# One GpSimd product placed later and one normalization given to ScalarE in a hand-ordered linear-attention and MLP kernel

## The chip, the cores and the metric

The kernel runs on one core of a Trainium2 chip. A core has a matrix engine (TensorE, in the profile PE, with its weight loads as PEld), a vector engine (VectorE, DVE), an activation engine (ScalarE, ACT), a general engine (GpSimd, POOL) and a queue that issues the DMA transfers (SyncE, SP). Each engine takes its instructions strictly in the order in which they stand in its own queue, and waits at an instruction until what that instruction needs is there. The metric is the device time of one execution in microseconds (us).

## The reference, cut to what matters

The input is a sequence of 2048 rows of 512 numbers. It goes through a linear attention with 32 heads of 16, and then through a block of two mixers, each with its own layer norm:

```python
h = _layernorm(x) * (1 + ca) + sa
q, k, v = split(h @ wqkv)                       # 32 heads of 16
phi_q = concat(softmax(q @ w_phi), softmax(-(q @ w_phi)))
phi_k = concat(softmax(k @ w_phi), softmax(-(k @ w_phi)))
kv, z = phi_k^T v, sum(phi_k)
x = x + ga * ((phi_q kv) / (phi_q z)) @ wo
h = _layernorm(x) * (1 + cb) + sb
t = gelu(_layernorm(h) @ w1)                    # then four column groups shifted by +1, -1, +2, -2 rows
x1 = h + shifted(t) @ w2
x = x + gb * (x1 + gelu(_layernorm(x1) @ w3) @ w4)
```

## The kernel before

The 2048 rows are 16 tiles of 128 rows, and two tiles are a chunk of 256. All products run in float32 precision, each as three products of a rounded part ("hi") and a rest ("lo"). The program has three phases. The first makes the features of keys, values and queries, chunk by chunk, and writes the exponentials of the queries to DRAM. The second (`phase_a` and `mix`, chunk by chunk) reads these exponentials back, divides and scales them, multiplies them with the sum over the keys (`num`), multiplies with `wo`, normalizes, multiplies with `w1`, shifts, and multiplies with `w2`. The third is the wide MLP with `w3` and `w4` in blocks of 512 rows, by a scheme of Strassen's kind with seven products in place of eight.

The body of the program only makes a list of numbered steps. The sequence in which they are issued is written out by hand in the string `ORDER`: each word is a step's number, and a letter behind it says that the step runs on another engine than the one it was written for (G is GpSimd, V is VectorE, A is ScalarE). `Plan.order` reads it:

```python
for word in ORDER.split():
    o = self.ops[int(word.rstrip("AVG"))]
    if not word.isdigit():
        o.fn = o.alts[engines[word[-1]]][1]
    yield o
```

An engine's queue is what is left of this string when one keeps the words of that engine. Buffers are given out by hand too (`SLOT`): a step that fills a buffer waits until the last reader of what was in it before is done.

The steps that matter here, with their numbers in `ORDER` and the line of their code:

- In `q_phi`, tiles 10 and 11 of the queries' exponentials. VectorE makes the factors of both tiles (1234, line 943, `q<-q,pz`). Tile 11's exponentials are scaled by them on VectorE (1237, line 947, `e<-e,q`), tile 10's on GpSimd (1235, same line, same name). VectorE then transposes each of them in blocks (1238 for tile 11, 1236 for tile 10, `pT<-e`), 1236 writing into the buffer from which 1238 reads. Between these two stands 1066, the lo part of a transposed normalized chunk (`nT<-pt,nT`), whose TensorE transposes (`pt<-const,n`) come just before the `num` products of chunk 5 (`pp<-pT,const`).
- GpSimd's queue at that place: a power of -1/2 for a layer norm (1056, line 586, `rs<-mv,const`), the product of 512 columns of w4 with the row gb (1485, line 1129 in `load_w4`, `raw<-raw,gb`), 1235, two lo parts of w3 (1220 and 988, line 483, `ws`), and tile 12's product with the sum over the keys (1307, line 932, `ez<-e,const`), which is written into the buffer from which 1236 reads. The next step that reads the w4 product is a rounding on ScalarE (1492), far behind.
- In `layernorm2` (line 621), called by `normed(0)`: the first layer norm of the MLP, in which two tiles are normalized with their scale and shift and written in a mixed column order. One of the two is on ScalarE (1575), the other on VectorE (1574, `nb<-xl,rs,nm`), behind the transpose of tile 13's exponentials (1319) and in front of the block transpose of its own result (1576, `yt<-nb`). Behind that stand the factors of tiles 14 and 15 (1392 to 1396, `pz` and `q`) and the lo part of chunk 6's attention output (1323, `oT<-pp,oT`), which TensorE multiplies with `wo` (1327, 1328, `pp<-w,oT`).
- ScalarE's queue at that place: the GELUs of chunk 4, one of their roundings (1180, `sh<-gf`), a sum for the next layer norm (1584, `nb<-xl`), a square sum (1258, `n<-pp,nm`) and a small step (1585, `nm<-st`), which writes into the buffer of the scale that 1574 reads.

In the profile, L415 and L417 are a two-operand step on VectorE and on GpSimd, L398 is a step on ScalarE, L407 is the same scaling step on VectorE or GpSimd, L468 are the products, L477 the transposes of TensorE, and L691 the block transposes of VectorE.

Of the kernel before, what the change touches and what calls it, by code (L numbers as in the profile page):

```python
# [37 lines left out]
        "c2": ("st", "mv", "rs", "nm"), "c64": ("k1", "k2", "q1", "q5"), "c128": ("q2", "q3")}  # L38
TAG = {n: tag for tag, names in KIND.items() for n in names}
ORDER = (  # L40
# [1394 lines left out]
```

## Time and profile before

| | |
|---|---|
| time, median of 3 executions | 553.92 us (553.47 to 554.73) |
| the profiled execution, its own time | 556.63 us |
| its span, first to last instruction | 554.8 us |
| mean granted TensorE clock | 0.996 of full speed |
| busy share of the span: VectorE, ScalarE, GpSimd | 89%, 62%, 67% |
| DMA read and written | 89.74 MB, 34.35 MB |

The span is shorter than the time of the same execution by 1.83 us, which lie ahead of the first and behind the last instruction. In the rows of the profile a name such as `pp<-w,oT` is "written from read", by the program's names of the buffers; the number ahead of it is the start in us from the first instruction, then the duration in us; in brackets stands how long the engine had been idle and which instruction ended that.

### The profile page before, as it was taken

How to read it: one execution, taken by the hardware profiler on the slowest of the kernel's cores; microseconds unless marked ns; L12 is line 12 of the kernel's file. 1: busy time of each engine (PE TensorE's matmuls, PEld its weight loads, DVE VectorE, ACT ScalarE, POOL GpSimd, SP SyncE). 2: the span in 40 equal slices, each digit the busy share in tenths (PEclk: the TensorE clock that was granted, in tenths of full speed). 3: DMA queues.
4: the chain of work that ended last, by engine and by line, in shares of the span. 5: the costliest groups of instructions: out<-in, count | busy, mean ns of one | idle time of the engine just before them, and what ended most of it. 6: DMA issues, size and time to landing. Idle time of an engine off the chain costs nothing.

```text
span 554.8 us, 12326 instructions
## 1 busy us (share of the span) xinstructions
PE 544.5 (98%) x4509; PEld 487.4 (88%) x4509; DVE 495.5 (89%) x895; ACT 344.0 (62%) x807; POOL 371.9 (67%) x383
## 2 busy tenths in 40 slices
PE   9999999999999999899899999999999999999997
PEld 8788788888777887788689898999999999999997
DVE  4899999999999999999989987988889877988787
ACT  3799988844337888777788577874534345234430
POOL 3588977979699999889786265433665563345354
PEclk9999999999999999999899999999999999999999
DMA  8967155158545668856797899997659674592032
GB/s 308 385 219 259 78 191 175 50 167 272 146 121 191 229 205 278 281 186 217 239 294 277 296 312 332 372 365 247 273 128 420 230 278 160 171 344 113 1 116 76
DMA packets 64180, 124.89 MB, mean 225 GB/s; under 512 B 7060, under 2 KB 26772, under 8 KB 60024
## 3 DMA queue, kind: packets, MB, share of 16 engines
q1 hardware_dynamic: 63688, 123.91, 65.4%
q8 instruction: 35, 0.57, 0.4%
q10 hardware_dynamic: 432, 0.20, 0.1%
q14 instruction: 25, 0.20, 0.1%
HBM read 89.74 MB, written 34.35 MB: 224 GB/s over the span
## 4 chain that ended last, share of the span: by engine, by line
PE 48%; POOL 11%; DVE 10%; issue 2%; ACT 1%; DMA 1%; POOLq 0%; DVEq 0%; SPq 0%
PE pa L468 23%; PE ac L468 17%; PE pp L468 7%; POOL ez L417 3%; POOL e L417 3%; POOL qe L417 2%; DVE pT L691 1%; DVE pz L439 1%; DMA dram<-ws 1%; POOL ws L417 1%; DVE xb L415 1%; POOL rs L586 1%; DVE e L415 1%; DVE nb L407 1%; POOL sh L417 1%
## 5 line engine op out<-in xcount | busy, mean ns | idle before, releaser
L468 PE MATMUL pp<-w,hh 128*128 128x512 f32 x576 | 137.4, 396 | 0.2 <-DVE hh L415 0.2
L468 PEld LDWEIGHTS pp<-w,hh 128*128 128x128 f32 x576 | 106.9, 188 | 25.5 <-issue 1.0
L468 PE MATMUL pa<-bH,wq 128*128 128x256 f32 x840 | 105.5, 281 | 0.0
L468 PE MATMUL ac<-w,gg 128*128 128x256 f32 x840 | 105.4, 281 | 0.0
L468 PEld LDWEIGHTS ac<-w,gg 128*128 128x128 f32 x840 | 102.8, 188 | 1.2
L468 PEld LDWEIGHTS pa<-bH,wq 128*128 128x128 f32 x840 | 102.3, 188 | 0.6
L468 PE MATMUL pp<-w,oT 128*128 128x512 f32 x192 | 48.8, 405 | 1.8 <-DVE q L415 1.8
L417 POOL TENSOR_TENSOR gg<-cu,gg 128x128 fp32r<-128x128 f32 (+1 forms) x32 | 22.4, 707 | 39.6 <-PE ac L468 14.1
L468 PE MATMUL pp<-w,sh 128*128 128x512 f32 x192 | 48.3, 398 | 0.0
L468 PE MATMUL pa<-nT,w 128*128 128x256 f32 x384 | 47.0, 281 | 0.0
L468 PEld LDWEIGHTS pa<-nT,w 128*128 128x128 f32 x384 | 46.1, 188 | 0.8 <-issue 0.2
L468 PEld LDWEIGHTS pp<-w,oT 128*128 128x128 f32 x192 | 36.3, 193 | 10.4 <-ACT nb L398 2.2
L468 PEld LDWEIGHTS pp<-w,sh 128*128 128x128 f32 x192 | 35.3, 189 | 8.5 <-issue 0.8
L398 ACT ACTIVATE cu<-pa 128x512 f32<-128x512 f32 (+1 forms) x41 | 21.3, 524 | 29.7 <-PE pa L468 12.8
L586 POOL TENSOR_TENSOR rs<-mv,const 128x2 f32<-128x2 f32 x31 | 23.9, 770 | 18.3 <-ACT mv L593 18.0
L417 POOL TENSOR_TENSOR ez<-e,const 128x1024 f32<-128x1024 f32 x12 | 29.5, 2461 | 5.3 <-DVE pT L691 4.2
L398 ACT ACTIVATE gg<-cu 128x256 fp32r<-128x256 f32 (+1 forms) x48 | 16.5, 360 | 25.1 <-PE ac L468 22.6
L415 DVE TENSOR_TENSOR gg<-sg,gg 128x512 fp32r<-128x512 f32 x36 | 26.4, 738 | 4.1 <-ACT gg L398 2.9
L417 POOL TENSOR_TENSOR e<-e,q 128x1024 f32<-128x1024 f32 x15 | 29.2, 1969 | 0.0
L398 ACT ACTIVATE gg<-sg 128x512 fp32r<-128x512 f32 x28 | 17.3, 625 | 18.4 <-PE ac L468 6.8
L417 POOL TENSOR_TENSOR ke<-ke,k 128x1024 f32<-128x1024 f32 x14 | 28.4, 2025 | 0.0
L415 DVE TENSOR_TENSOR cu<-pa,cu 128x512 f32<-128x512 f32 (+1 forms) x36 | 21.0, 594 | 7.5 <-PE pa L468 5.8
(220 smaller groups left out, 1238.1 us busy)
## 6 DMA issues: line engine op xcount, KB each, us to landing
wq<-dram SPq DMA_DIRECT2D x32, 1024.0 KB, 8.2
dram<-ws SPq DMA_DIRECT2D x35, 256.0 KB, 3.5
dram<-qe SPq DMA_DIRECT2D x16, 512.0 KB, 3.0
e<-dram SPq DMA_DIRECT2D x64, 128.0 KB, 3.3
xl<-in_x SPq DMA_DIRECT2D x30, 256.0 KB, 4.5
raw<-in_w SPq DMA_DIRECT2D x18, 256.0 KB, 4.1
mod<-in_wmod SPq DMA_DIRECT2D x16, 256.0 KB, 4.7
dram<-xl SPq DMA_DIRECT2D x16, 256.0 KB, 3.0
```

The costliest lines, as they stand in the source:

```text
L398: nc.scalar.activation(o(), i(), func, **kw)
L407: other.append((e, c, lambda eng=eng: eng.tensor_scalar(o(), i(), get(s1), get(s2), op0=OP.mult, op1=OP.add), not isps(i) and not isps(o)))
L415: dve = ("DVE", 71 + 1.04 * o.n + 90 * (isps(a) and isps(b)), lambda: nc.vector.tensor_tensor(o(), a(), b(), op=op))
L417: pool = ("Pool", cost, lambda: nc.gpsimd.tensor_tensor(o(), a(), b(), op=op))
L439: plan.op("DVE", 65 + 1.04 * a.n + 110 * isps(o), lambda: nc.vector.tensor_reduce(o(), a(), axis=AX.X, op=op), [o], [a])
L468: nc.tensor.matmul(o(), a(), b(), start=s, stop=e, **kw)
L586: plan.op("Pool", 540 + 10 * m, lambda: nc.gpsimd.tensor_tensor(r(), v(), mhalf[:, :m](), op=OP.pow), [r], [v, mhalf])
L691: plan.op("DVE", 71 + 1.04 * o.n, lambda: nc.vector.transpose(o(), i()), [o], [i])
```

## The change

Only the string `ORDER` changes. Word by word many numbers trade places, but most of them do so across engines. Kept apart by engine, TensorE's and the DMA queue have the same sequence as before, and three queues differ by two moves:

- GpSimd: 1485, the w4 product, stood between 1056 and 1235. Now it stands behind 1235, 1220 and 988, and in front of 1307.
- VectorE and ScalarE: 1574, the normalization, loses its V. It is gone from VectorE between 1319 and 1576, and stands on ScalarE between 1180 and 1584.

```diff
-    "1090G 1230 874 1231 1055 1113 1108 1056 1232 1137 1114 1145 1485G 1058 600 1233 1063 995 1234 1139 1057 1237 "
-    "1059 1235G 1238 1064 1140 1065 1066 1220G 1236 1146 961 988G 965 1141 1307G 989 1060 1239 1305 1061 1240 1213 "
...
+    "1090G 1230 874 1231 1055 1113 1108 1056 1232 1137 1114 1145 1058 600 1233 1063 995 1234 1139 1237 1057 1059 "
+    "1235G 1238 1064 1140 1065 1066 1220G 1236 1146 961 988G 965 1141 1485G 989 1060 1305 1239 1061 1240 1213 1307G "
...
-    "1076 1075 1216 1183 1493G 1319 1175 1579 1083 1250 1179 1084 1180 1574V 1488G 1584 1576 1085 1258 1486G 1392 "
...
+    "1075 1216 1183 1493G 1319 1175 1579 1083 1179 1250 1084 1180 1488G 1085 1574 1486G 1086 1584 1576 1217G 1258 "
```

26 rows, old and new, of the table ORDER are left out of this document.

## The prediction

> **What bounds the kernel now.** I read the page first, then TensorE's waits, the windows around the two longest, and there the timelines of the engines.
>
> ```profile
> span 554.8 us, 12326 instructions
> PE 544.5 (98%) x4509; PEld 487.4 (88%) x4509; DVE 495.5 (89%) x895; ACT 344.0 (62%) x807; POOL 371.9 (67%) x383
> ```
> ```profile
> PE pt L477 <- DVE nT L415: 2.3, 1, 2.3
> PE pp L468 <- DVE q L415: 1.8, 1, 1.8
> ```
> ```profile
> 269.98:273.40 3.42, 1.60 (x8) 0.86 (x7) 3.35 (x9) 2.62 (x10) 1.61 (x3) 1.00 0.89 290
> 273.40:276.81 3.41, 3.41 (x10) 2.59 (x9) 3.41 (x8) 2.85 (x6) 3.41 (x4) 0.50 1.11 270
> ```
>
> TensorE is busy 98% of the span, and two waits, both for VectorE, make up most of the rest. In the windows around the second wait (stretch, its length, then the busy times of PE, PEld, DVE, ACT, POOL, then the granted clock) TensorE is busy 1.60 us of 3.42 in the first, and the clock is 0.50 in the next. So a TensorE wait can be paid twice. The change touches just these two places.
>
> **Tile 10.** VectorE's, GpSimd's and TensorE's queues there:
>
> ```profile
> 229.58 0.29 DVE L415 TENSOR_TENSOR q<-q,pz 128x128 f32<-128x128 f32 x1
> 229.90 4.58 DVE L415 TENSOR_TENSOR e<-e,q 128x1024 f32<-128x1024 f32 x1
> 234.51 1.25 DVE L691 STREAM_TRANSPOSE pT<-e 128x1024 f32<-128x1024 f32 x1
> 235.68 0.65 DVE L415 TENSOR_TENSOR nT<-pt,nT 128x512 fp32r<-128x512 f32 x1
> 236.26 1.23 DVE L691 STREAM_TRANSPOSE pT<-e 128x1024 f32<-128x1024 f32 x1
> ```
> ```profile
> 227.92 0.92 POOL L586 TENSOR_TENSOR rs<-mv,const 128x2 f32<-128x2 f32 x1
> 228.81 1.29 POOL L417 TENSOR_TENSOR raw<-raw,gb 128x512 f32<-128x512 f32 x1
> 230.07 1.93 POOL L417 TENSOR_TENSOR e<-e,q 128x1024 f32<-128x1024 f32 x1
> 231.97 0.73 POOL L417 TENSOR_TENSOR ws<-wr,ws 128x256 fp32r<-128x256 f32 x1
> 232.67 0.73 POOL L417 TENSOR_TENSOR ws<-ws 128x256 fp32r<-128x256 f32 x1
> 237.56 2.39 POOL L417 TENSOR_TENSOR ez<-e,const 128x1024 f32<-128x1024 f32 x1 [4.17 <-DVE pT L691]
> ```
> ```profile
> 231.03 3.01 PE L468 MATMUL pp<-w,oT 128*128 128x512 f32 x12
> 236.39 0.66 PE L477 MATMUL pt<-const,n 128*128 128x128 f32 x4 [2.34 <-DVE nT L415]
> 237.54 1.16 PE L468 MATMUL pp<-pT,const 64*32 64x128 f32 x64 [0.49 <-DVE pT L691]
> ```
> ```profile
> 246.34 1.22 DVE L415 TENSOR_TENSOR ez<-e,const 128x1024 f32<-128x1024 f32 x1
> ```
>
> VectorE's scaling of tile 11 takes 4.58 us; a product of the same size takes 1.22 (the last row). It starts while GpSimd is in the w4 product, and ends 1.08 us after GpSimd's run of four ends (232.67 + 0.73 = 233.40, against 234.48): VectorE stood outside until GpSimd paused. The Trainium skill, page "SBUF — State Buffer", section "Who interferes with whom", has the rule: a VectorE instruction with two SBUF inputs and a GpSimd instruction that reads SBUF block each other, and the second waits until the first finishes. The trace agrees that they block each other, but not on the length: by the rule the wait would have ended with the w4 product at 230.10, and it lasted three instructions more.
>
> In the changed queue GpSimd is idle from 228.84. Its scaling and VectorE's are released by the same instruction, which ends at 229.58 + 0.29 = 229.87. VectorE goes on at 229.90. GpSimd began 0.07 after VectorE in the one case of the rows above (237.56 after 236.26 + 1.23), so at 229.94. Who comes first by so little?
>
> ```profile
> 528.81 0.68 DVE L415 TENSOR_TENSOR xb<-xb,uu 128x512 f32<-128x512 f32 x1
> 528.83 0.98 POOL L417 TENSOR_TENSOR gg<-cu,gg 128x128 fp32r<-128x128 f32 x1
> ```
> ```profile
> 246.56 1.60 POOL L417 TENSOR_TENSOR ws<-ws 128x256 fp32r<-128x256 f32 x1
> ```
>
> With 0.02 of lead VectorE ran undisturbed and GpSimd's small product was drawn out. With 0.22 of lead (246.34 above, and 246.56) GpSimd's `ws` took 1.60 in place of 0.73. So I let VectorE win: tile 11 is scaled at 229.90 + 1.22 = 231.12, transposed at 232.37, `nT` done at 233.0. GpSimd scales tile 10 from 231.12 to 233.05, VectorE transposes it by 233.05 + 1.23 = 234.28. TensorE is done with its twelve products at 231.03 + 3.01 = 234.04 and finds `nT` there; its transposes move up to that end, and `pp<-pT` starts at about 234.35 in place of 237.54: **3.2 us** earlier. Both waits go.
>
> What is late next is GpSimd, whose idle 4.17 us paid for everything. Now `ws`, `ws` and the w4 product (0.73 + 0.73 + 1.29) run to 235.80, and `ez` starts there, only 1.76 earlier than before.
>
> ```profile
> 244.02 0.70 POOL L586 TENSOR_TENSOR rs<-mv,const 128x2 f32<-128x2 f32 x1 [0.39 <-ACT mv L593]
> ```
>
> The row is the next place where GpSimd had time to spare, 0.39. It gets there 1.76 + 0.39 = 2.15 earlier, while ScalarE's moments are there 3.2 earlier; VectorE read the result 0.28 after its end (its row starts at 245.00, by the dense order of its queue). I carry 2.15 + 0.25 = **2.4 us** on from here. The product itself is late for nobody: its reader, a rounding on ScalarE, stands more than 30 us behind it, and its DMA isn't moved.
>
> **The normalization.**
>
> ```profile
> 264.24 4.48 DVE L407 TENSOR_SCALAR nb<-xl,rs,nm 128x512 f32<-128x512 f32 x1
> 268.76 0.71 DVE L691 STREAM_TRANSPOSE yt<-nb 128x512 f32<-128x512 f32 x1
> ...
> 272.06 0.68 DVE L415 TENSOR_TENSOR oT<-pp,oT 128x512 fp32r<-128x512 f32 x1
> ```
> ```profile
> 263.29 1.33 POOL L417 TENSOR_TENSOR w<-raw,w 128x512 fp32r<-128x512 f32 x1
> ...
> 267.31 1.12 POOL L417 TENSOR_TENSOR sh<-gf,sh 128x512 fp32r<-128x512 f32 x1
> ```
> ```profile
> 264.84 0.61 ACT L398 ACTIVATE nb<-xl 128x512 f32<-128x512 f32 x1
> ...
> 268.82 0.20 ACT L593 ACTIVATE nm<-st 128x2 f32<-128x2 f32 x1 [2.60 <-DVE nb L407]
> ```
> ```profile
> 267.41 3.05 PE L468 MATMUL pp<-w,sh 128*128 128x512 f32 x12
> 272.29 4.65 PE L468 MATMUL pp<-w,oT 128*128 128x512 f32 x12 [1.82 <-DVE q L415]
> ```
> ```profile
> L398 ACT ACTIVATE nb<-xl,nm,rs x11: 800/815/822, 260.2 to 370.9; 128x512 f32<-128x512 f32 x11
> L407 DVE TENSOR_SCALAR nb<-xl,rs,nm x4: 510/541/4483, 264.2 to 310.7; 128x512 f32<-128x512 f32 x4
> ```
>
> It is the same picture: 4.48 us where the group's median is 0.54, from inside GpSimd's `w` (the first of six instructions without a pause) to 0.29 after the last (267.31 + 1.12 = 268.43). On ScalarE the step costs 0.82 by its eleven like ones. In the times of before, ScalarE would run it from 264.84 to 265.66; VectorE, which now has nothing to scale, waits for it and starts `yt` at about 265.7, **3.05** earlier than 268.76. The steps behind it on ScalarE slide by 0.72 (0.82 less the usual overlap of 0.1), but the 2.60 wait of `nm` goes, since the buffer that it takes is then freed by ScalarE itself: 266.95 in place of 268.82, **1.9** earlier. `yt` no longer blocks or is blocked: the transposes ran beside GpSimd at their usual 0.7 and 1.2.
>
> TensorE would be free at 267.41 + 3.05 = 270.46 and finds `oT` there (272.06 + 0.68 - 3.05 = 269.7): the 1.82 wait goes. Its twelve products took 4.65, the like ones 3.01; the difference of 1.64 is the stretch of half clock in the third window. If the gap goes, that goes: 1.82 + 1.64 = **3.46 us**. The Trainium skill has this gate in "TensorE: Matmul & The Clock Gate", section "What's actually happening": half clock comes after at least one idle window of about 3.4 us. The trace's window before the halving was not idle but 1.60 busy of 3.42, so here half a window did it; by the rule the halving wouldn't belong to the gap, and the 1.64 would stay.
>
> What could eat some of it: ScalarE and GpSimd come only 1.9 ahead, and if TensorE hung on them all the way, the part would be 1.9, a loss of 1.56; if on VectorE alone, nothing.
>
> ```profile
> 284.08 0.60 ACT L398 ACTIVATE oT<-pp 128x512 fp32r<-128x512 f32 x1 [0.47 <-PE pp L468]
> ```
>
> By here ScalarE waits for TensorE again and can catch up, so I take 0.4, near the lower end.
>
> **The sum** against the profiled execution: 2.4 + 3.46 - 0.4 = 5.46, say 5.4 us; its span would be 549.4 and its time 556.63 - 5.4 = 551.2. TensorE has no wait of any length behind 272, and the chain there is TensorE alone, fed by what it makes itself and by transfers issued in step, so I expect the gain to last to the end. The profiled execution stands 2.71 above the median of the timed ones, 553.92; I take the same difference off that: **548.5 us**.
>
> **Rivals.**
>
> *GpSimd wins the start at tile 10 but nothing more* (0.10). It then keeps VectorE out for 1.93 + 0.73 + 0.73 + 1.29 from 229.94 to 234.62, and VectorE ends at 234.62 + 1.08 = 235.70, 1.2 later than before; the second part still gives 3.46: 553.92 + 1.2 - 3.46 = 551.7. For it: the lead is 0.04 only.
>
> *Slower: that start with a half clock behind it* (0.07). TensorE's gap grows from 2.34 to 3.5, the window that follows is then emptier than the one that halved the clock, and another 1.64 is paid. If in the timed executions the later halving stays, or wasn't there, the second part gives 1.82 only: 553.92 + 1.2 + 1.64 - 1.82 = 554.9. It decides at 229.94 against 229.90.
>
> *No change: the timed executions lack the long stand-outs* (0.12). If a blocked VectorE instruction waits for one GpSimd instruction only, 229.90 would have waited 0.2 and 264.24 0.38; TensorE's waits would be gone already, and both moves are worth nothing: 553.9, within 0.3. Against it: the profile has two that outlast three and five instructions, and its time is only 0.5% above the median. The wait for one instruction is the port rule of the Trainium skill, "SBUF — State Buffer", "Who interferes with whom".
>
> *The half clock stays although the gap goes* (0.06): 5.4 - 1.64 = 3.8, 550.1. That is the clock rule of the Trainium skill's page on TensorE, named above.
>
> **Chances.** The forecast has 0.65: both waits and the half clock go. Its own range is 5.4 with 1.6 less (the loss above in full is 1.16 more; GpSimd's lateness another 0.4) and up to 7.0 (the 3.2 carried on in full and no loss give 6.7; VectorE's 3.05 + 2.4 ahead of need the rest): 546.9 to 550.1. The range must take in 551.7 too and a forecast that is half lost, so 546.9 to 552.6, with the two cases above that left out. About 0.2% (1.1 us) is what a measurement of this kernel can tell from no change. Faster by more: 0.65 + 0.10 + 0.06 = 0.81; within: 0.12; slower: 0.07.
>
> **What would show it.** Right: `e<-e,q` of VectorE at 1.2 to 1.3 us with GpSimd's behind it; no TensorE wait for `nT` or `q`; `nb<-xl,nm,rs` twelve times on ScalarE; no stretch of 0.5 behind 265. Wrong: a VectorE instruction of 3 us or more anywhere (then the blocking has only moved), GpSimd's `e` ahead of VectorE's, `rs` or `ez` of GpSimd named in TensorE's chain, or the same TensorE span from the first `wq` products on with the gain gone before.

## The result, and the profile after

| | before | after |
|---|---|---|
| time, median of 4 executions | 553.73 us (553.47 to 554.73) | 549.74 us (549.55 to 549.88) |
| ratio, 95% interval | | 0.9924 (0.9907 to 0.9941) |
| the profiled execution, its own time and span | 556.63, 554.8 us | 549.88, 548.1 us |

The change takes 4.0 us off the median. Between the two profiles it takes 6.7 us. That these two numbers differ is the main thing to be explained.

The page of the profile after begins so:

```profile
span 548.1 us, 12324 instructions
...
PE 542.3 (99%) x4509; PEld 486.4 (89%) x4509; DVE 488.4 (89%) x894; ACT 344.3 (63%) x808; POOL 373.5 (68%) x383
```

TensorE's waits after (line waited, for whom, total, times, longest):

```profile
PE pp L468 <- POOL const L495: 1.0, 1, 1.0
PE pt L477 <- ACT n L398: 0.6, 2, 0.3
PE pp L468 <- POOL sh L1053: 0.3, 1, 0.3
```

The waits for `nT` and `q` are gone; one of 0.3 for GpSimd is new. At tile 10, VectorE's, GpSimd's and TensorE's timelines after (start, duration, instruction):

```profile
229.23 1.22 DVE L415 TENSOR_TENSOR e<-e,q 128x1024 f32<-128x1024 f32 x1
230.49 1.25 DVE L691 STREAM_TRANSPOSE pT<-e 128x1024 f32<-128x1024 f32 x1
231.66 0.65 DVE L415 TENSOR_TENSOR nT<-pt,nT 128x512 fp32r<-128x512 f32 x1
```
```profile
229.27 2.98 POOL L417 TENSOR_TENSOR e<-e,q 128x1024 f32<-128x1024 f32 x1 [1.11 <-DVE q L415]
...
233.62 1.28 POOL L417 TENSOR_TENSOR raw<-raw,gb 128x512 f32<-128x512 f32 x1
234.86 2.40 POOL L417 TENSOR_TENSOR ez<-e,const 128x1024 f32<-128x1024 f32 x1
```
```profile
230.37 3.01 PE L468 MATMUL pp<-w,oT 128*128 128x512 f32 x12
233.21 0.60 PE L477 MATMUL pt<-const,n 128*128 128x128 f32 x4
233.74 1.16 PE L468 MATMUL pp<-pT,const 64*32 64x128 f32 x64
```

VectorE leads GpSimd by 0.04 and is done after 1.22; GpSimd's scaling is the one that is drawn out (2.98). TensorE's transposes follow its products without a gap. At the normalization, in the timelines of ScalarE, VectorE and TensorE after:

```profile
261.66 0.80 ACT L398 ACTIVATE nb<-xl,nm,rs 128x512 f32<-128x512 f32 x1
```
```profile
262.49 0.71 DVE L691 STREAM_TRANSPOSE yt<-nb 128x512 f32<-128x512 f32 x1 [1.36 <-ACT nb L398]
```
```profile
264.18 3.05 PE L468 MATMUL pp<-w,sh 128*128 128x512 f32 x12
267.06 2.97 PE L468 MATMUL pp<-w,oT 128*128 128x512 f32 x12
```

VectorE now waits 1.36 for ScalarE, and it costs nothing: TensorE's twelve products start where the ones before them end and take 2.97 in place of 4.65.

Both traces hold the same 4509 matmuls in the same order, so the start of one and the same matmul can be compared. Where the difference changes:

| matmul | before | after | difference |
|---|---|---|---|
| `pp<-bd,rk`, first phase | 11.01 | 10.39 | 0.62 |
| `pt<-const,n`, tile 10 | 236.39 | 233.21 | 3.18 |
| `pp<-pT,const` | 237.54 | 233.74 | 3.80 |
| `pp<-w,sh` | 250.40 | 247.19 | 3.22 |
| `pp<-w,oT`, behind the normalization | 272.29 | 267.06 | 5.22 |
| `pp<-w,sh`, behind those twelve | 276.73 | 269.87 | 6.86 |
| end of the last matmul | | | 6.74 |

0.62 is there before the change begins. Tile 10 gives 3.80 - 0.62 = 3.18, of which 0.58 is given back by 250, all of it where TensorE now waits 0.30 for GpSimd's `sh` and at the matmul behind that; the normalization gives 6.86 - 3.22 = 3.64, of which 2.0 is the wait and 1.64 the half clock.

### The profile page after: what moved, and what is told of

It is laid out like the page before. It is cut to its first block, busy times and chain, and to the rows that moved or that the text cites. A ratio compares the mean times of both kernels' runs of the same rounds, so it can differ in the third digit from the quotient of the medians.

```text
span 548.1 us, 12324 instructions
## 1 busy us (share of the span) xinstructions
PE 542.3 (99%) x4509; PEld 486.4 (89%) x4509; DVE 488.4 (89%) x894; ACT 344.3 (63%) x808; POOL 373.5 (68%) x383
## 4 chain that ended last, share of the span: by engine, by line
PE 52%; POOL 12%; DVE 5%; issue 3%; DMA 1%; SPq 1%; POOLq 0%; DVEq 0%
PE pa L468 24%; PE ac L468 18%; PE pp L468 10%; POOL ez L417 3%; POOL ws L417 2%; POOL qe L417 2%; POOL e L417 2%; POOL sh L417 1%; DMA e<-dram 1%; POOL rs L586 1%; DVE pz L439 1%; DVE xb L415 1%; DVE gg L415 1%; PE pt L477 1%; POOL w L417 0%
## 5 line engine op out<-in xcount | busy, mean ns | idle before, releaser
L468 PE MATMUL pp<-w,oT 128*128 128x512 f32 x192 | 47.1, 395 | 0.0
```

The source lines that it names most:

```text
L468: nc.tensor.matmul(o(), a(), b(), start=s, stop=e, **kw)
```

## The experiments

Two theories stood at the start. A: every execution of before has both long instructions of VectorE and the half clock, and the profiled one was longer for another reason. B: the executions of before differ in which of these losses they have.

### The kernel before, again

No edit.

> The kernel before, unchanged. The profiled execution of before (556.63 us) stood 2.9 above the timed median (553.73), the one of after (549.88) 0.1. Theory A (every execution of before has both long stand-outs of VectorE and the half clock, the profile is merely slower elsewhere): a second profile shows 4.58 and 4.48 us again, mean clock below 0.998 in every execution, and the difference to 553.7 lies in rows outside 228 to 277 us. Theory B (the executions of before differ in which of the three losses they have): times in steps, about 556.6 with all three, 555.0 without the half clock (1.64), 553.2 to 553.4 without one of the stand-outs; a clock of 1.000 in the executions near 553.5 shows that the half clock is what they lack.

Measured: 553.93 us (549.37 to 557.47, 12 executions), ratio to before 0.9992 (0.9965 to 1.0018). The profiled one took 553.38, with a span of 551.6. VectorE's timeline at the two places:

```profile
229.04 4.57 DVE L415 TENSOR_TENSOR e<-e,q 128x1024 f32<-128x1024 f32 x1
...
264.56 0.71 DVE L407 TENSOR_SCALAR nb<-xl,rs,nm 128x512 f32<-128x512 f32 x1
```

The first block is there, the second isn't. TensorE's timeline behind the first, and the windows there (stretch, length, busy times of PE, PEld, DVE, ACT, POOL, granted clock):

```profile
235.52 0.66 PE L477 MATMUL pt<-const,n 128*128 128x128 f32 x4 [2.32 <-DVE nT L415]
236.67 1.96 PE L468 MATMUL pp<-pT,const 64*32 64x128 f32 x64 [0.49 <-DVE pT L691]
```
```profile
232.78:236.19 3.41, 1.07 (x6) 0.42 (x4) 3.38 (x4) 0.68 (x2) 0.00 (x0) 1.00 0.63 207
236.19:239.61 3.42, 2.94 (x67) 2.36 (x68) 3.36 (x7) 1.79 (x4) 2.91 (x2) 0.50 0.24 57
239.61:243.02 3.41, 3.41 (x29) 3.36 (x28) 2.98 (x4) 3.38 (x10) 2.93 (x5) 1.00 0.20 74
```

Here the half clock follows the first gap: `pp<-pT` takes 1.96 in place of 1.16. Matmul by matmul, this execution falls behind the changed kernel by 3.16 in the gap and by 1.25 in the half clock, wins back 0.65, and was 0.23 ahead before: 3.5 in all, as the spans say (551.6 and 548.1).

Theory B holds in its main point, that the executions differ in their losses, but not in its steps: it expected a clock of 1.000 near 553.5, and there it is about 0.996, which the second profile explains: the half clock is paid behind the first gap. The 69 executions of before in this study, beside the four of the first comparison, fall into groups: one at 549.37 (clock 0.999, not profiled), four at 552.1 to 552.4 with a mean clock of 0.999 or 1.000, 37 at 553.3 to 554.8 (clock 0.995 to 0.997), and 27 at 555.4 to 557.5 (clock 0.994 to 0.997). The first profile was one of the last group, the four executions that it was compared with are of the third. Which losses stand behind a group is read from its times and clocks; only two executions of before were profiled.

### The GpSimd move alone

```diff
-... 1145 1485G 1058 ... 1141 1307G 989 ...
+... 1145 1058 ... 1141 1485G 1307G 989 ...
```

> Only the w4 product of GpSimd is moved, the normalization stays on VectorE. Theory A: tile 11's scaling takes 1.2 us with GpSimd's tile 10 behind it, TensorE's wait of 2.34 goes, 2.4 to 3.2 us faster than before: 550.5 to 551.3. Theory B with the first stand-out missing in the timed executions: 553.7, no change. Theory B with the second missing: close to the full change, 549.7 to 550.5. In all of them the second stand-out (normalization on VectorE, 4.48) may come at another moment against GpSimd, since both engines come earlier by unequal amounts; if it then finds a gap, the time is that of the full change.

> The GpSimd move alone once more, for the profile of an execution of its slow group (9 of 12). If it is slow, theory N shows the normalization at over 2 us on VectorE and a TensorE wait for q or oT behind 265; theory S shows GpSimd's scaling of tile 10 ahead of VectorE's of tile 11 at 229 and VectorE's at 4 us or more.

> The same again, a second chance for a slow execution; expectations as for the one before.

Measured: 552.83 us, ratio 0.9966 (0.9946 to 0.9986), in two groups: three executions at 549.6 to 550.2, nine at 552.2 to 553.8. Two further profiled executions took 552.89 and 552.76. The three profiles agree at tile 10 (VectorE's scaling 1.22 or 1.23, no TensorE wait) and differ at the normalization. VectorE and GpSimd in the first one (549.58):

```profile
260.87 0.65 DVE L407 TENSOR_SCALAR nb<-xl,rs,nm 128x512 f32<-128x512 f32 x1
```
```profile
259.91 1.33 POOL L417 TENSOR_TENSOR w<-raw,w 128x512 fp32r<-128x512 f32 x1
261.17 0.94 POOL L417 TENSOR_TENSOR tw<-raw,raw 128x256 f32<-128x256 f32 x1
```

and in the second profile (552.89), with TensorE:

```profile
261.62 4.49 DVE L407 TENSOR_SCALAR nb<-xl,rs,nm 128x512 f32<-128x512 f32 x1
```
```profile
260.66 1.33 POOL L417 TENSOR_TENSOR w<-raw,w 128x512 fp32r<-128x512 f32 x1
261.92 0.77 POOL L417 TENSOR_TENSOR tw<-raw,raw 128x256 f32<-128x256 f32 x1
```
```profile
269.67 2.17 PE L468 MATMUL pp<-w,oT 128*128 128x512 f32 x8 [1.88 <-DVE q L415]
```

In both, VectorE comes 0.96 behind the start of GpSimd's `w`. In one it got in at the next boundary (and GpSimd's `tw` was drawn out to 0.94), in the other it missed it and stood outside for five instructions more. The third profile has 4.50, again at 0.96. So the upper group is the normalization's (theory N), and GpSimd winning the start (theory S) was in none of the three. In the four profiles in which both engines have this part as before (two are of runs further below), VectorE got in at 0.87, 0.89 and 0.94 (0.71, 0.71 and 0.65 long) and missed at 0.95 (4.48, the first profile): the edge lies near 0.95, and to the hundredth it isn't sharp.

### The ScalarE move alone

```diff
-... 1084 1180 1574V 1488G ...
+... 1084 1180 1574 1488G ...
```

> Only the normalization is given to ScalarE, the w4 product stays in front of GpSimd's scaling. Theory A: the 4.58 at 229.9 stays, the wait of 1.82 and the half clock behind it go: 553.7 - 3.5 = 550.2, at least 553.7 - 1.8 = 551.9 if the half clock was not there in timed executions. Theory B with the second stand-out missing in the timed executions: 553.7, no change; with the first missing: the full gain, 549.7.

Measured: 553.28 us (552.41 to 553.97), ratio 0.9974 (0.9954 to 0.9993). In its profile VectorE's scaling at tile 10 took 4.58. Five executions lie at 552.4 to 552.8 with a clock of 0.999 or 1.000, seven at 553.1 to 554.0 with 0.995 to 0.997: the first gap without and with the half clock. None lies above 554.0, where 42 of the 69 of before do, 27 of them above 555. So this move takes away the upper tail; the median it moves by 1.0 us only. Nearest is theory B with the second block missing: it is missing in most executions of before, and the move takes it from the rest.

### The normalization on VectorE, one place earlier

```diff
-... 1493G 1319 ... 1180 1574V 1488G ...
+... 1493G 1574V 1319 ... 1180 1488G ...
```

> The normalization stays on VectorE, one place earlier: in front of the transpose of tile 13 (at 263.1 in the times of before), where GpSimd is in a short cast of 0.2 us and not yet in its run of six. GpSimd's w4 product unmoved. Theory of the port (what costs 4.48 is only the moment at which the instruction comes, not that VectorE has it to do): it takes 0.5 to 0.9 us and the time is that of the ScalarE move alone within 0.6 us. Rival (VectorE is short of time there, the step itself has to go): the transposes and factors behind it come 0.6 later or the block falls on it all the same (4 us or more), and the time stays within 0.5 of before.

> The w4 product moved as in the change, the normalization kept on VectorE but one place earlier, in front of the transpose of tile 13. The GpSimd move alone gave two groups, 549.6 to 550.2 (3 of 12) and 552.2 to 553.8 (9 of 12). Theory N (the slow group comes from the normalization being kept out by GpSimd's run of six): one group at 549.5 to 550.2, the slow one gone. Theory S (it comes from GpSimd winning the start at tile 10): both groups again, in about the same shares.

Alone: 553.76 us (553.32 to 556.53), ratio 0.9993 (0.9976 to 1.0009); the normalization took 0.52, and the time is within 0.5 of that of the ScalarE move. It can't be told from before either, as the rival had it, so this run alone doesn't decide; the next one does. With the GpSimd move: 550.76 us (549.96 to 550.91, 6 executions), ratio 0.9912 (0.9890 to 0.9934), one group; the upper group, nine of twelve, is gone. Four of the six lie above the 550.2 that theory N expected, and the median is 0.85 above that of the changed kernel measured beside it (549.91). In the profile 0.60 of the 0.92 by which the span is longer than after stand in the first phase; the rest stays open. VectorE and GpSimd in that profile:

```profile
260.56 1.78 DVE L407 TENSOR_SCALAR nb<-xl,rs,nm 128x512 f32<-128x512 f32 x1
```
```profile
260.76 1.30 POOL L417 TENSOR_TENSOR w<-raw,w 128x512 fp32r<-128x512 f32 x1
263.64 0.74 POOL L417 TENSOR_TENSOR tw<-raw,raw 128x256 f32<-128x256 f32 x1 [1.58 <-DVE pT L691]
```

VectorE came 0.20 ahead of `w`, but GpSimd was already in a run of three casts (from 260.36). It stood outside for the rest of the casts and for `w`, and was let in when that ended (262.06), since GpSimd's next instruction had to wait for VectorE. The step can stay on VectorE; what costs is the moment at which it comes and how long GpSimd's run behind that is.

The profile of the first of the two (555.33) shows that the half clock, too, comes in sizes. Its windows:

```profile
233.08:236.49 3.41, 1.07 (x7) 0.52 (x5) 3.38 (x4) 0.79 (x2) 0.00 (x0) 1.00 0.76 266
236.49:239.90 3.41, 2.92 (x68) 2.32 (x67) 3.41 (x7) 1.66 (x4) 2.77 (x2) 0.50 0.18 42
239.90:243.32 3.42, 3.42 (x16) 3.23 (x16) 2.72 (x5) 3.39 (x9) 2.93 (x5) 0.50 0.16 60
```

Two windows at 0.50 in place of one. With the same gap, the span is 1.9 us longer than in the second profile of before, of which 0.43 was there in the first phase and 1.3 came in the second window. Its mean clock is 0.994, and eight of the 27 above 555 have that clock too; so these may not need the second block. The other 19 have 0.995 to 0.997, like the first profile (0.996).

### The changed kernel, again

No edit.

> The changed kernel again, for the spread of its executions: four so far lie between 549.55 and 549.88. Theory (the change takes away both places at which VectorE can be kept out, and with them what makes executions of before differ by 8 us): all within 0.5 of 549.7, clock 0.999 or 1.000. Rival (GpSimd wins the start at tile 10 in some of them): a second group at 552 to 554.

Measured: 549.91 us (549.50 to 550.48, 6 executions), ratio to the executions of before measured beside it 0.9901 (0.9878 to 0.9925). Two of the six, at 550.30 and 550.48, lie beyond the expected 0.5 of 549.7. With the first four, ten executions lie within 1.0 us, where those of before spread over 8.2. No second group. Those of before had a median of 555.59 here: six of the eleven were of the upper group, so the same change was worth 5.7 us.

### A shorter and a longer run of GpSimd

The first takes one `ws` (1220) out of GpSimd's run behind the w4 product, past its pause; the second puts one `w` (1481) in front of that pause. All else is the kernel before.

```diff
-... 1220G 1236 1146 961 988G 965 1141 1307G 989 ...
+... 1236 1146 961 988G 965 1141 1307G 1220G 989 ...
```
```diff
-... 961 988G 965 ... 1142 1481G 1067 ...
+... 961 988G 1481G 965 ... 1142 1067 ...
```

> The kernel before with one lo part of w3 (1220, ws, 0.73) taken out of GpSimd's run of four behind the w4 product and put behind the next ez, past GpSimd's pause. Theory P (VectorE is let in only when GpSimd pauses, once it has missed the first boundary): tile 11's scaling takes 4.58 - 0.70 = 3.88 and TensorE's wait for nT falls from 2.34 to about 1.6. Rival F (VectorE waits a fixed time, or tries again after a fixed one): 4.58 again. Rival R (each boundary between two GpSimd instructions is a new chance): shorter by one or two whole instructions, 1.4, 3.1 or 3.9 by chance.

> The kernel before with GpSimd's next w product (1481, w, 1.02), which waits for nothing, put in front of the ez that makes GpSimd pause: its run behind the w4 product gets longer by one instruction. Theory P: tile 11's scaling takes 4.58 + 1.0 = 5.6, TensorE's wait for nT grows from 2.34 to 3.3. Rival F: 4.58 and 2.34 as before. Rival R: 4.58 or less.

Measured, VectorE and TensorE in the shorter run (552.34 us, one execution):

```profile
229.78 3.88 DVE L415 TENSOR_TENSOR e<-e,q 128x1024 f32<-128x1024 f32 x1
```
```profile
235.58 0.66 PE L477 MATMUL pt<-const,n 128*128 128x128 f32 x4 [1.65 <-DVE nT L415]
```

and in the longer run (554.55 us, one execution), with GpSimd's last instruction ahead of its pause:

```profile
229.41 5.55 DVE L415 TENSOR_TENSOR e<-e,q 128x1024 f32<-128x1024 f32 x1
```
```profile
232.87 1.01 POOL L417 TENSOR_TENSOR w<-raw,w 128x384 fp32r<-128x384 f32 x1
```
```profile
236.87 0.90 PE L477 MATMUL pt<-const,n 128*128 128x128 f32 x4 [3.32 <-DVE nT L415]
```

With three, four and five instructions in GpSimd's run VectorE's takes 3.88, 4.58 and 5.55, and TensorE waits 1.65, 2.34 and 3.32. In the longer run VectorE ends at 234.96, again 1.08 after GpSimd (233.88). Theory P has both sizes, and a fixed wait (F) has neither. A new chance at each boundary (R) allowed 3.9 in the shorter run, but nothing above 4.58 in the longer one. Each size stands on one execution.

### The product in GpSimd's gap

The changed kernel, with 1485 between 1101 and 1170:

```diff
-... 1141 1485G 989 ... 1101G ... 1170G ...
+... 1141 989 ... 1101G ... 1485G 1170G ...
```

> The changed kernel with the w4 product further behind: between GpSimd's ws at 246.0 and its normalization n at 247.9, where it stood idle for 1.22 in the changed kernel. The ez of tile 12 then starts 1.25 earlier, and the small cast (sh) that TensorE waited 0.30 for at 245 comes that much earlier. Theory: that wait goes, 0.3 faster than the changed kernel, 549.4 to 549.6, which can hardly be told from it. Rival (GpSimd's earlier ws or sh now meets VectorE at another phase and keeps it out): 551 or more, with a VectorE instruction of over 2 us.

Measured: 550.15 us (549.75 to 550.56, 6 executions), ratio to before 0.9916 (0.9886 to 0.9947), against 0.9924 and 0.9901 for the changed kernel. The wait of 0.3 for GpSimd's `sh` went, and there came another. VectorE, GpSimd and TensorE's waits:

```profile
246.38 2.28 DVE L415 TENSOR_TENSOR ez<-e,const 128x1024 f32<-128x1024 f32 x1
```
```profile
246.28 1.30 POOL L417 TENSOR_TENSOR raw<-raw,gb 128x512 f32<-128x512 f32 x1
247.58 1.73 POOL L407 TENSOR_SCALAR n<-h,rs,nm 128x512 f32<-128x512 f32 x1
```
```profile
PE pp L468 <- DVE nT L415: 0.7, 1, 0.7
```

GpSimd started 0.10 ahead of VectorE's product and kept it out for 1.06 (2.28 for 1.22). It is the rival in kind, with an instruction of over 2 us, though not in its time of 551 or more: VectorE stood outside for one GpSimd instruction only. No run's median is below those of the changed kernel.

## Why the prediction was right or wrong

The forecast was 548.5 and the measured time 549.74, within its range; the gain was 4.0 where 5.4 was forecast.

**Who comes first at tile 10: right.** VectorE at 229.23, GpSimd at 229.27: the 0.04 that the prediction worked out. The rival that GpSimd wins the start was seen neither in the ten executions of the changed kernel, all within 1.0 us, nor in any of the seven profiles with the product behind the scaling: VectorE leads by 0.04 or 0.05 in each and takes 1.22 or 1.23.

**The sizes at tile 10: right.** 3.2 forecast, 3.18 measured. The reason why less is carried on was right too: GpSimd is late next. Its `ez` starts 5.63 behind VectorE's scaling (234.86 - 229.23; 5.90 forecast), and TensorE then waits 0.30 for GpSimd's `sh`. 3.18 - 0.58 = 2.60 is carried, where 2.4 was taken.

**The normalization, in the profiled executions: right, a little low.** 0.80 on ScalarE (0.82 forecast), both the wait and the half clock gone, 3.64 measured against 3.46 less 0.4. The deduction wasn't needed: no wait of TensorE for ScalarE or GpSimd appears there. Between the profiles the change is so worth 6.74, of which 0.62 lies in the first phase.

**The last step of the sum: wrong.** "The profiled execution stands 2.71 above the median of the timed ones ... I take the same difference off that". This carries a gain found in one execution over to others that don't have the same losses. The profiled execution had the second block with the half clock behind it; the usual one, by the times and clocks of the 37 above, has no second block, and a half clock behind the first gap (1.25 in the second profile of before). What the timed executions gained was therefore the first gap and its half clock, 3.16 + 1.25 - 0.65 - 0.23 = 3.5 by the spans of two such executions, of the 4.0 between the medians, and not 2.4 + 3.46 - 0.4. That the forecast came near is in part luck: the half clock, which it booked at the second place, is usually paid at the first.

**The rival of no change: half right.** It said that timed executions lack the long blocks. The first block stands in all six profiles of a kernel that has the product in front of the scaling. The second stands in one of the four among them that leave the normalization as it was; in the other three VectorE waited for one instruction only, which is the rival's mechanism. Against it stood that the profile "is only 0.5% above the median"; that distance was the sign that the two weren't alike.

**The parts seem not to add.** Alone they give 0.34% and 0.26%, together 0.99% or, in the first set of executions, 0.76%; with the intervals above, the excess over the sum is not clear for the 0.76 and barely for the 0.99. The groups say why one should be there: in those two runs one gap left is enough for 552.2 to 554.0, against 549.5 to 550.5 without any, and after the GpSimd move alone eleven of fourteen executions were of the upper group.

**The clock.** The prediction read that a window half idle is enough for the half clock. The windows lie in steps of 3.41 us, as the traces' records of the granted clock show: in the first profile of before full clock is on record from 7.18 and the half clock from 273.42, 78 steps behind. Two more windows show the edge, in the first profile of before at tile 10 and, counted in the same steps from 6.38, in the shorter run, each with the one behind it:

```profile
232.46:235.87 3.41, 1.59 (x7) 0.95 (x6) 3.38 (x3) 1.84 (x3) 0.93 (x2) 1.00 0.79 306
235.87:239.29 3.42, 2.41 (x71) 1.89 (x72) 3.42 (x8) 1.46 (x4) 1.73 (x1) 1.00 0.49 134
```
```profile
231.66:235.07 3.41, 2.27 (x10) 1.50 (x8) 3.38 (x3) 2.50 (x4) 0.92 (x2) 1.00 0.91 359
235.07:238.49 3.42, 2.42 (x71) 1.89 (x72) 3.42 (x8) 1.47 (x4) 1.74 (x1) 1.00 0.55 162
```

Windows busy for 1.07 of 3.41, and the one of 1.60 at 270 in the first profile, were followed by 0.50; those of 1.59 and 2.27 were not. So the edge lies near half a window, and the modelled busy time doesn't place it more closely. The half clock lasted two windows where the first of them was busy for 2.92, and one where it was busy for 2.94; why stays open. The Trainium skill, "TensorE: Matmul & The Clock Gate", "What's actually happening", says that the window runs free and doesn't reset with the kernel. The runs fit that: the same gap of 2.3 us was followed by no, one or two windows of half clock, and the windows lay on it differently. The rival that the half clock stays although the gap goes didn't occur: the ten executions of the changed kernel have a mean clock of 0.999 or 1.000.

## What to carry to other kernels

Where a two-operand or scaling instruction of VectorE can start while GpSimd is at work on operations like those here, look at how long GpSimd runs from there without a pause: that whole run can be the price, not one instruction. Let VectorE lead while GpSimd is idle, or break the run, or give the step to ScalarE. Before a gain read from one profile is booked, check that the profile's own time lies among the timed ones; if it stands apart, ask which of its losses the others have, and take several profiles. A change that takes away a race is worth more in some sets of executions than in others (4.0 and 5.7 us here), so its size needs many executions of before.

## What the runs showed of the hardware

In these runs a VectorE instruction that missed the first boundary between two GpSimd instructions was kept out until GpSimd paused: 3.88, 4.58 and 5.55 us by the length of the run. The Trainium skill, "SBUF — State Buffer", "Who interferes with whom", has the blocked one wait until the other instruction finishes; the first profile of the GpSimd move alone agrees (0.65), the other two don't (4.49, 4.50). What decides between the two at the same offset of 0.96 stays open; the rows of the two engines just ahead of that point don't tell these executions apart.

The same program had executions 8.2 us apart on one core. Where profiles show the spread, it stands mostly in two rows of VectorE and in where the windows of TensorE's clock fell; the fastest and the slowest execution were not profiled.
